# One more set of first-layer tiles by half products, and partial sums that grow in PSUM, in an attention and mixer kernel

## The chip, the core and the metric

The kernel runs on one core of one Trainium2 chip. The metric is device time in microseconds (us): the median of three runs is 332.39 us (332.39 to 332.7). A profiled execution of its own took 332.49 us, and its trace spans 330.7 us. TensorE multiplies (weights are loaded, then a matmul streams columns through them), VectorE, ScalarE and GpSimd work elementwise, SyncE issues DMAs. TensorE writes only to PSUM, which has eight banks of 512 f32 columns; GpSimd does not touch PSUM here.

## The reference: what is computed

Eight batches of 576 tokens and eight heads of 64 channels: causal attention, with 16 beacon keys ahead that every token sees; then a low-rank mix over the tokens, and a two-layer MLP over the channels.

```python
scores = scale * np.matmul(q, k_all.transpose(0, 1, 3, 2))
scores = np.where(causal, -1000000000.0, scores)
a = np.exp(scores - scores.max(-1, keepdims=True)); a /= a.sum(-1, keepdims=True) + 1e-09
x = np.matmul(a, v_all)                     # then (B, S, H * D): 8 x 576 x 512
u = x + ((x.transpose(0, 2, 1) @ U) @ V).transpose(0, 2, 1)
out = u + np.maximum(u @ w_ch1, 0.0) @ w_ch2   # 512 -> 2048 -> 512
```

## The kernel before

**Two streams of work.** The 4608 tokens are nine MLP blocks of 512 tokens, numbered 0 to 8; a block needs the mixed result `u` of the batch or batches that it lies in. Attention goes by pairs of heads. A *visit* makes scores (`sps`, L410: matmuls of 64 rows, two heads side by side) and ScalarE turns them into exponentials (L419); then come 15 matmuls per head against the values (`po`, L428), and VectorE takes the reciprocal of the sums (L436) and scales the head into `xb` (L437). After a batch's last head, DMA transposes and two small products (`qtp`, L465, four groups of 32 columns; `ups`, L490, 32 rows) make `u`, transposed, in the ring `uT`. MLP blocks are cut into *units* which wait in a queue; `fill(n)` takes `n` of them between pieces of attention. After the last batch the queue is emptied with no attention left.

**Who orders.** Nothing is scheduled: each engine carries out its instructions in the order in which the program issues them, and semaphores make it wait for operands and for buffers. PSUM tiles take the first bank of the list `emptied` (`pst`) and put it at the list's end when their last reader has been issued (`emptying`), so a bank is used again in the order in which banks were given back, and a matmul into it waits for that reader.

**A block.** The first layer has 16 output tiles `gT` of 128 channels by 512 tokens. A *plain* tile is four matmuls of 512 columns (`gps`, L675; in block 4, where the ring wraps, eight of 256) and a ReLU on ScalarE (L683) or VectorE (L681). A *set* makes four tiles (2q, 2q+1, 8+2q, 9+2q) at once by seven products of half channels by half tokens (a Strassen-Winograd scheme), each of four matmuls of 256 columns, 28 in all (`qps`, L701). Blocks 3 to 5 make one set, blocks 6 to 8 three (`PARTS`). The weights' sums for a set lie in freed staging tiles (`quad_weights`, L615, GpSimd); the sums of `u` are VectorE's (L603). In a set, bank A takes the first product, ScalarE copies it to SBUF (L720), A goes on to grow by the second, third and fourth product, with a copy after each; F takes a product alone and VectorE adds the copy (L723) and applies the ReLU (L728); D grows by two products and VectorE adds copies to it twice.

The second layer treats the whole block the same way: seven products of 16 matmuls of 256 columns, over sums of the tiles (`sums`, L653, VectorE). In blocks 1 to 6 products have banks A to F of their own (`product`, L829; A of blocks 3 to 6 by `grown`, L909), and VectorE adds each bank to the kept stage before it (`after`, L849); in blocks 7 and 8 one bank A grows. GpSimd adds `u` (L577), SyncE stores.

Of the kernel before, what the change touches and what calls it, by code (L numbers as in the profile page):

```python
# [11 lines left out]
F32 = mybir.dt.float32  # L12
# [6 lines left out]
P = 128  # L19
# [11 lines left out]
def kernel(  # L31
# [73 lines left out]
    bank_of = {}  # L105

    def pst(shape, dtype, name):

        b = emptied.pop(0)
        t = psum.tile(shape, dtype, tag=f"bank{b}", name=name)  # L110
        bank_of[id(t)] = (b, t)
        return t

# [467 lines left out]
    def quad_tiles(q):  # L581

        if q == 0:
            w = [pairs.tile([P, 512], F16, name=f"lw{k}", tag=f"pr{k % 2}") for k in range(4)]
        else:
            w = [staged[q - 1][:, ds(512 * k, 512)] for k in range(4)]
            f = staged[q + 1][:, 0 : 2048].bitcast(F32).rearrange("p (k i x) -> p k i x", k=2, i=2)
            lq["k", q] = (f[:, 0], f[:, 1], f[:, 0])
# [6 lines left out]
    def u_sums(t0, eng):  # L595

        b11, b12, b21, b22 = (u_half(t0, c, x) for c in (0, 2) for x in (0, HT))
        t1, t2, t3, t4 = (staged[i][:, 5 * DM : 6 * DM].rearrange("p (c x) -> p c x", c=2) for i in range(4))
        lq["t"] = [t1, t2, t3, t4]

        def one(o, x, y):
            assert (t0 + 511) // S in settled
            eng.tensor_tensor(out=o, in0=x, in1=y, op=ALU.subtract)  # L603
# [18 lines left out]
    def fast_units(t0, dst, last=False, parts=0, ahead=None):  # L622
# [3 lines left out]
        few = PARTS.get(t0 // 512 + 1, 0) == 1  # L626
# [3 lines left out]
        def begin():  # L630
            t = gtp.tile([P, NDC * 512 + 3 * HF * HT], F16, name="gT", tag="gT")
# [14 lines left out]
        def sums(i, d0, n):  # L646
# [6 lines left out]
            nc.vector.tensor_tensor(out=o[:, ds(d0, n)], in0=x[:, ds(d0, n)], in1=y[:, ds(d0, n)], op=op)  # L653

        order = [d + HF * h for d in range(HF) for h in range(2)]

        def g_unit(k):
            if k == 0:
                begin()


            def between():
                if k % 2 and cell["turns"]:
                    cell["turns"].pop(0)()
                for x in SUMS.get(k, ()):
                    sums(*x)

            layer_one(order[k], k in (2, 5, 11, 13), between)

        def layer_one(dc, on_vector, between=lambda: None):  # L670
# [8 lines left out]
            between()  # L679
            if on_vector:  # L680
                nc.vector.tensor_scalar_max(out=cell["g"][:, dc, :], in0=g, scalar1=0.0)  # L681
            else:
                nc.scalar.activation(out=cell["g"][:, dc, :], in_=g, func=AF.Relu)  # L683
            emptying(g)

        def g_quads():

            b11, b12, b21, b22 = (u_half(t0, c, x) for c in (0, 2) for x in (0, HT))
            us = u_sums(t0, nc.vector)
            t1, t2, t3, t4 = lq["t"]  # L690
            held = {}

            def plain(k, dc):
                layer_one(dc, parts == 1 and k in (2, 11, 13))

            def half(q, bank, a, b, fresh):
                if fresh:
                    held[q, bank] = pst([P, 2, HT], F32, name="qps" + bank)
                for i in range(2):
                    for c in range(2):  # L700
                        nc.tensor.matmul(  # L701
                            held[q, bank][:, i, :], a(c, i), b[:, c, :], start=fresh and i == 0 and c == 0,
                            stop=c == 1, skip_group_check=True,
                        )

# [3 lines left out]
            def of_lw(q, k):  # L709
                return lambda c, i: lq["w", q][k][:, c, ts(i, P)]  # L710

            def space(q, k):
                if k < 2:
                    cell["k", q, k] = lq["k", q][k] if q else kept("k")
                else:
                    cell["k", q, k] = cell["k", q, 0]
                return cell["k", q, k]

            def copied(q, k):
                nc.scalar.activation(out=space(q, k), in_=held[q, "A"], func=AF.Copy)  # L720
# [949 lines left out]
```

## Time and profile before

| what | number |
|---|---|
| median of three runs | 332.39 us |
| the profiled execution, and its span | 332.49 us, 330.7 us |
| TensorE busy | 322.6 us, 98% of the span, 3660 matmuls |
| VectorE busy | 264.7 us, 80% |
| ScalarE busy | 196.4 us, 59% |
| GpSimd busy | 166.7 us, 50% |
| granted TensorE clock, mean | 0.996 |
| plain tiles of 512 columns in blocks 1 to 8 (L675) | 272 matmuls, 66.3 us |

Busy shares are means over the span, and the end of a matmul is modelled. A row of the timeline gives the start, the length from the first start to the last end, the engine, line and operation, output and inputs, and a count; a row of the groups gives the count, the busy time and the mean length of one, and then the engine's idle time ahead of it with who ended it.

### The profile page before, as it was taken

The page shows a single profiled execution, that of the slowest core. Times are in us where ns is not written, and L with a number is a line of the kernel's source. Part 1 is how long each engine was busy: PE and PEld are TensorE (multiplying, and loading weights), DVE is VectorE, ACT ScalarE, POOL GpSimd, SP SyncE. Part 2 cuts the span into 40 slices and gives each one's busy share as a digit, 9 for nine tenths or more (in the row PEclk, how much of TensorE's full clock was granted, in tenths as well). Part 3 has the DMA queues.
Part 4 walks back from the last instruction along what each step waited for, and adds up shares of the span by engine and source line. Part 5 has one row for each costly group of instructions (what it writes and reads, how often), then busy time and mean ns, then how long its engine had stood idle before and what let it go on. Part 6 is the DMA issues. An engine that isn't in the chain of part 4 may idle for free.

```text
span 330.7 us, 9280 instructions
## 1 busy us (share of the span) xinstructions
PE 322.6 (98%) x3660; PEld 228.1 (69%) x3660; DVE 264.7 (80%) x608; ACT 196.4 (59%) x430; POOL 166.7 (50%) x263
## 2 busy tenths in 40 slices
PE   7899999999999999999999999999999999999994
PEld 3564555555578656876588888765787888788783
DVE  6776988679998668786878777877788898798993
ACT  5957962789972677348844695379636613703700
POOL 8987724766238960689058923950283036030030
PEclk9999999999999999999999999999999999999998
DMA  7999999999999996999999999995014313405003
GB/s 164 142 179 143 185 201 194 200 187 155 80 129 166 215 130 106 111 162 138 148 149 162 146 135 160 92 211 81 10 65 120 70 44 101 63 11 166 18 10 125
DMA packets 150561, 41.99 MB, mean 127 GB/s; under 512 B 131312, under 2 KB 149936, under 8 KB 150512
## 3 DMA queue, kind: packets, MB, share of 16 engines
q0 software_dynamic: 87568, 18.18, 73.1%
q1 hardware_dynamic: 62144, 22.41, 37.4%
q10 hardware_dynamic: 800, 0.75, 0.7%
q8 instruction: 30, 0.49, 0.7%
q14 instruction: 19, 0.16, 0.2%
HBM read 37.45 MB, written 9.44 MB: 142 GB/s over the span
## 4 chain that ended last, share of the span: by engine, by line
PE 91%; ACT 4%; DVE 1%; DMA 1%; issue 0%; ACTq 0%
PE gps L675 21%; PE mpsA L909 9%; PE po L428 8%; PE qpsA L701 6%; PE mpsD L829 6%; PE sps L410 6%; PE cps L1053 4%; PE gps L1027 4%; PE mpsE L829 3%; PE mpsC L829 3%; PE mpsB L829 3%; PE qpsD L701 3%; ACT expt L377 2%; PE mpsF L829 2%; PE mpsD L909 2%; ACT w L377 2%
## 5 line engine op out<-in xcount | busy, mean ns | idle before, releaser
L577 POOL TENSOR_TENSOR ob<-ob,ut 128x128 f32<-128x128 f32 x104 | 50.0, 511 | 121.9 <-DVE ob L849 59.4
L419 ACT ACTIVATE expt<-sps 128x496 f16<-128x496 f32 (+2 forms) x192 | 82.0, 539 | 41.8 <-PE sps L410 41.8
L675 PE MATMUL gps<-uT,w 128*128 128x512 f16 (+1 forms) x368 | 78.1, 351 | 0.0
L829 PEld LDWEIGHTS <-gT 128*128 128x128 f16 x576 | 54.2, 98 | 8.8 <-issue 2.6
L675 PEld LDWEIGHTS <-w 128*128 128x128 f16 x368 | 33.2, 98 | 25.6 <-issue 1.3
L653 DVE TENSOR_TENSOR gT<-gT 128x1024 f16<-128x1024 f16 (+3 forms) x87 | 47.0, 561 | 0.9
L239 POOL DMA_DIRECT2D vs<-in_v_dram x50 | 39.9, 811 | 14.1 <-DMA w<-in_moe_w_ch_dram 11.6
L683 ACT ACTIVATE gT<-gps 128x512 f16<-128x512 f32 x63 | 37.4, 617 | 16.1 <-PE gps L675 11.9
L428 PEld LDWEIGHTS <-expt 128*128 128x128 f16 x900 | 33.9, 98 | 8.4 <-issue 1.5
L428 PE MATMUL po<-vs,expt 128*128 128x65 f16 x900 | 36.4, 194 | 0.6 <-DVE expt L349 0.4
L909 PEld LDWEIGHTS <-gT 128*128 128x128 f16 x336 | 31.2, 98 | 4.0
L437 DVE TENSOR_TENSOR xb<-po,rec 128x320 f16<-128x320 f32 x64 | 31.4, 491 | 2.2
L349 DVE TENSOR_TENSOR expt<-expt,bigmask 128x768 f16<-128x768 f16 x56 | 31.3, 598 | 0.4 <-ACT expt L419 0.2
L720 ACT ACTIVATE kept<-qpsA 128x512 f32<-128x512 f32 x18 | 10.9, 603 | 24.0 <-PE qpsA L701 13.2
L410 PE MATMUL sps<-qT,kT 64*128 64x80 f16 (+4 forms) x288 | 22.6, 281 | 0.0
L436 DVE RECIPROCAL rec<-po 128x5 f32<-128x5 f32 x64 | 11.9, 186 | 12.4 <-PE po L428 12.1
L377 ACT ACTIVATE expt<-sps 128x496 f16<-128x496 f32 (+2 forms) x48 | 20.6, 572 | 0.6 <-PE sps L371 0.6
L909 PE MATMUL mpsA<-w,gT 128*128 128x256 f16 x160 | 19.1, 273 | 0.0
L410 PEld LDWEIGHTS <-kT 64*128 64x128 f16 x288 | 10.2, 94 | 12.8 <-issue 8.2
L681 DVE TENSOR_SCALAR gT<-gps 128x512 f16<-128x512 f32 x17 | 11.7, 688 | 8.5 <-PE gps L675 8.2
L1126 POOL DMA_DIRECT2D st<-in_k_dram x20 | 16.9, 860 | 1.4 <-DVE xb L437 1.4
L1126 POOL DMA_DIRECT2D st<-in_q_dram x20 | 17.0, 877 | 0.2 <-DVE expt L349 0.2
(159 smaller groups left out, 540.4 us busy)
## 6 DMA issues: line engine op xcount, KB each, us to landing
out_dram<-ob SPq DMA_DIRECT2D x33, 256.0 KB, 3.4
vs<-in_v_dram POOLq DMA_DIRECT2D x18, 128.0 KB, 7.2
w<-in_moe_w_ch_dram POOLq DMA_DIRECT2D x4, 512.0 KB, 6.6
w<-in_moe_w_ch_dram POOLq DMA_DIRECT2D x2, 1024.0 KB, 13.1
st<-in_k_dram POOLq DMA_DIRECT2D x12, 128.0 KB, 6.3
st<-in_q_dram POOLq DMA_DIRECT2D x12, 128.0 KB, 8.3
st<-in_k_dram POOLq DMA_DIRECT2D x4, 288.0 KB, 11.5
st<-in_q_dram POOLq DMA_DIRECT2D x4, 288.0 KB, 12.5
```

The costliest lines, as they stand in the source:

```text
L239: nc.gpsimd.dma_start(out=dst[a : a + nq[j], j, :, :], in_=src[hs, ds(q0[j], nq[j]), :].rearrange("h p d -> p h d"))
L377: nc.scalar.activation(out=ex[i][:, ds(AT[g], gw[g])], in_=ps[g, i][:, 0 : gw[g]], func=AF.Exp, scale=scale)
L410: nc.tensor.matmul(banks[i][:, ds(at0 + o, w)], kT(hp, c, ch), qT[hp, c, ds(qa, w)], start=True, stop=True, skip_group_check=len(unit) > 1,)
L419: nc.scalar.activation(out=at[p][3][i][:, ds(AT[g], gw[g])], in_=bank[:, ds(at0, gw[g])], func=AF.Exp, scale=scale)
L428: nc.tensor.matmul(po[:, j, :], ex[0 : nk[c], ds(blk[(c, j)], P)], vs[0 : nk[c], ds(c * H * E + h * E, E)], start=(c == 0), stop=(c == j),)
L577: nc.gpsimd.tensor_tensor(out=o[:, i, ds(c, w)], in0=x[:, i, ds(c, w)], in1=y[:, i, ds(c, w)], op=op)
L653: nc.vector.tensor_tensor(out=o[:, ds(d0, n)], in0=x[:, ds(d0, n)], in1=y[:, ds(d0, n)], op=op)
L675: nc.tensor.matmul(g[:, ds(o, w)], w1[:, cc, ts(dc, P)], uT[:, cc, ds(at, w)], start=(cc == 0 and o == 0), stop=(cc == NCC - 1), skip_grou ...
L683: nc.scalar.activation(out=cell["g"][:, dc, :], in_=g, func=AF.Relu)
L829: nc.tensor.matmul(ps, a()[:, d, ds(P * i, P)], bm[:, d, ds(c0, w)], start=fresh and d == 0 and i == 0, stop=d == HF - 1, skip_group_check ...
L909: nc.tensor.matmul(ps, a()[:, d, ds(P * i, P)], bm[:, d, ds(c0, w)], start=fresh and d == 0, stop=d == HF - 1, skip_group_check=True,)
L1126: coming.append(lambda d=dst, s=src, a=m[j] - nq[j], n=m[j], j=j: nc.gpsimd.dma_start(out=d[a:n, j, :, :], in_=s[:, ds(q0[j], nq[j]), :].r ...
```

## The change

1. **Sets.** Blocks 3 to 5 make sets 0 and 3, blocks 6 to 8 make all four. Set 3 keeps its weight sums in the quarter of `w2` (first half of the rows, second half of the columns) that nothing reads after block 0; the rarely taken general branch loads that quarter again.
2. **Seeds.** `pst(..., onto=True)` takes a free bank that matmuls have filled whole before. ScalarE copies the first product of A into it and F's product is added onto it there, so VectorE's addition is gone. Where no such bank is free, the old way stays. In the program as built this holds for 13 of 18 sets and for the second layer of blocks 1 to 6.
3. **Second layer of blocks 1 to 6.** One bank A grows by four products, as blocks 7 and 8 do; ScalarE copies whole stages of 512 columns out of A to the output tiles, D is added to them by VectorE. B, C and E are gone.
4. **Order.** A table of words per block (`PLANS`) gives each unit its steps, the sums, the transposes and the engine of each copy or ReLU; a table per batch (`SLOTS`) gives the order of attention and units from batch 3 on.

```diff
+    def pst(shape, dtype, name, onto=False):
+        n = next(i for i, b in enumerate(emptied) if b in filled) if onto else 0
+        b = emptied.pop(n)
...
+            def a(q, eng):
+                x = half(q, "A", of_w1(0, 2 * q), b11)
+                if seedable():
+                    held[q, "F"] = pst([P, 2, HT], F32, "qpsF", True)
+                copy(eng, held[q, "F"] if (q, "F") in held else space(q, 1), x)
+            def f(q, eng):
+                onto, c11 = (q, "F") in held, low(2 * q)
+                x = half(q, "F", of_w1(2, 2 * q), b21)
+                if not onto:
+                    summed(c11, x, k[q, 1])
+                relu(eng if onto else "v", c11, x if onto else c11)
+                freed(q, "F")
+            def b(q, eng):
+                copy(eng, space(q, 0), half(q, "A", of_lw(q, 1), t2))
+            def d(q, eng):
+                half(q, "D", of_lw(q, 0), t1)
+            def c(q, eng):
+                copy(eng, space(q, 1), half(q, "A", of_lw(q, 2), t3))
+                summed(high(HF + 2 * q), held[q, "D"], k[q, 1])
+            def e(q, eng):
+                relu(eng, low(HF + 2 * q), half(q, "A", of_w1(2, HF + 2 * q), t4))
+                freed(q, "A")
+            def g(q, eng):
+                summed(high(2 * q), half(q, "D", of_lw(q, 3), b22), k[q, 0])
+                freed(q, "D")
...
-            elif k == 2:
-                add(kept("u2"), banks["B"], cell["s1"])
-                freed("B")
...
+            def one(i):
+                grown(0, "A", i, 0, HC)
+                if i:
+                    cell["onto"] = seedable()
+                    if cell["onto"]:
+                        banks["F"] = pst([P, 2, HC], F32, "mpsF", True)
+                    copied(banks["F"] if cell["onto"] else kept("s1"), "A")
+            def six(i):
+                grown(2, "A", i, 0, HC)
+                if i:
+                    copied(out_tile("12"), "A")
...
-    PARTS = {3: 1, 4: 1, 5: 1, 6: 3, 7: 3, 8: 3}
+    PLANS = {
...
+            g1 | e0 r0 | r1s | g2 +0.0.4 | d3 c3 +1.1.1 t1 e2 t1 | r2p +1.0.1 | e1 m0 e3 t1 g3 r3 | m1 +0.4.2
...
+    SLOTS = {
...
+            t f v1:2,1:1,1:0 y f f a0 b0 f f m1 v2:0,2:1,2:2 l f f f a1 f y f y b1 f f f L f f v2:3,3:0,3:3,3:1
```

The order lists three places on which the prediction speaks. A `MATMUL` row stands here for all that are like it; rows between are left out at "...".

First, TensorE at the end of the fourth batch, in block 3 (`gT_2940` before, `gT_2934` now): the last head `po`, twelve score matmuls, and what follows. Before:

```order
L428 MATMUL po_3099<-vs0_111,expt3_108 128x65
L410 MATMUL sps0_3122<-qT_2559,kT1_110 128x336
...
L410 MATMUL sps1_3135<-qT_2559,kT1_110 128x208
L675 MATMUL gps_3148<-uT_102,w1_93 128x512
L675 MATMUL gps_3154<-uT_102,w1_93 128x512
```

Now:

```order
L436 MATMUL po_3092<-vs0_111,expt3_108 128x65
L418 MATMUL sps0_3115<-qT_2557,kT1_110 128x464
...
L418 MATMUL sps1_3126<-qT_2557,kT1_110 128x80
L704 MATMUL qpsA_3144<-uT_102,w1_93 128x256
L704 MATMUL qpsD_3151<-st0_113,w2_94 128x256
L685 MATMUL gps_3156<-uT_102,w1_93 128x512
```

A plain tile stood behind the scores; now the new set's first product stands there, and the bank that it takes is the one of the head just ahead, so its first weight load waits for VectorE's `xb`. Blocks 4 and 5 have the same place.

Second, TensorE where the last set's bank A grows, in block 6. Before (third set, `qpsA_5020`):

```order
L701 MATMUL qpsA_5020<-st1_114 128x256
L675 MATMUL gps_5049<-uT_102,w1_93 128x512
L701 MATMUL qpsA_5020<-st2_115,st1_114 128x256
L701 MATMUL qpsD_5061<-st0_113,st1_114 128x256
L909 MATMUL mpsA_5068<-w2_94,gT_4835 128x256
L701 MATMUL qpsA_5020<-st3_116,w1_93 128x256
L701 MATMUL qpsD_5061<-uT_102,st1_114 128x256
```

Now (set 3, `qpsA_5052`; the fourth product of set 2, `qpsA_4939`, lies between):

```order
L704 MATMUL qpsA_5052<-st1_114,w2_94 128x256
L704 MATMUL qpsF_5057<-uT_102,w1_93 128x256
L704 MATMUL qpsA_5052<-st2_115,w2_94 128x256
L818 MATMUL mpsA_5094<-w2_94,gT_4851 128x256
L704 MATMUL qpsA_4939<-st3_116,w1_93 128x256
L704 MATMUL qpsD_5059<-uT_102,w2_94 128x256
```

Between the second and the third product into A stood a plain tile of 512 columns; now four matmuls of 256 stand there. In block 4 it is the mixer's `qtp` that stands at this place:

```order
L704 MATMUL qpsA_3804<-st1_114,w2_94 128x256
L473 MATMUL qtp_3856<-xb_3226,Usb_95 32x128
L704 MATMUL qpsA_3804<-st2_115,w2_94 128x256
L685 MATMUL gps_3886<-uT_102,w1_93 128x256
L436 MATMUL po_3897<-vs0_111,expt0_105 128x65
```

Before, those twenty `qtp` came straight behind a visit of scores.

Third, ScalarE in the second layer of block 3. Before, with both halves of a stage copied apart:

```order
L919 ACTIVATE kept_3296<-mpsA_3287 128x256
L919 ACTIVATE kept_3296<-mpsA_3299 128x256
L419 ACTIVATE expt0_105<-sps0_3311 128x496
...
L419 ACTIVATE expt1_106<-sps1_3320 128x496
L926 ACTIVATE ob_3341<-mpsA_3287 128x256
L926 ACTIVATE ob_3341<-mpsA_3299 128x256
```

Now:

```order
L893 ACTIVATE mpsF_3321<-mpsA_3301 128x512
L427 ACTIVATE expt0_105<-sps0_3327 128x496
...
L427 ACTIVATE expt1_106<-sps1_3340 128x464
L893 ACTIVATE ob_3366<-mpsA_3301 128x512
L893 ACTIVATE ob_3454<-mpsA_3301 128x512
L893 ACTIVATE ob_3465<-mpsF_3321 128x512
```

The first stage is now copied whole and into PSUM, ahead of the six exponentials of the visit that stands between the first and the second product into A; three more stages of A and F follow as copies of ScalarE.

563 lines of the change are left out of this document (259 added, 304 removed), and 3 rows, old and new, of the table SUMS.

## The prediction

> **What bounds the kernel now.** I read the page's first, second and fourth parts, and then asked the trace for TensorE's waits.
>
> ```profile
> PE 322.6 (98%) x3660; PEld 228.1 (69%) x3660; DVE 264.7 (80%) x608; ACT 196.4 (59%) x430; POOL 166.7 (50%) x263
> PE   7899999999999999999999999999999999999994
> PE 91%; ACT 4%; DVE 1%; DMA 1%; issue 0%; ACTq 0%
> PE idle L274 <- DVE ones L159: 1.2, 1, 1.2
> PE sps L371 <- DVE qT L332: 0.5, 1, 0.5
> PE tps L299 <- DVE pr L292: 0.5, 2, 0.3
> PE po L428 <- DVE expt L349: 0.4, 1, 0.4
> PE po L428 <- DVE w L349: 0.2, 1, 0.2
> ```
>
> TensorE is busy in every slice but the first and the last, it holds 91% of the chain, and all its waits that are long enough to be listed come to 2.8 us in lines that run in the first two batches. Busy alone proves little, because matmul ends are modelled: a wait under about 0.16 us can hide in the tail of the matmul before. So I looked at the steps between matmuls in the timeline.
>
> ```profile
> 121.31 3.63 PE L675 MATMUL gps<-uT,w 128*128 128x512 f16 x16
> 163.85 1.91 PE L909 MATMUL mpsA<-w,gT 128*128 128x256 f16 x16
> 165.69 0.79 PE L410 MATMUL sps<-qT,kT 64*128 64x496 f16 x10
> 166.42 0.28 PE L909 MATMUL mpsA<-w,gT 128*128 128x256 f16 x1
> L675 PE MATMUL gps<-uT,w 128*128 128x512 f16 x272 | 66.3, 379 | 0.0
> L909 PE MATMUL mpsA<-w,gT 128*128 128x256 f16 x160 | 19.1, 273 | 0.0
> ```
>
> Sixteen matmuls of 512 columns take 3.63 us and the last of them 0.379, so one follows another after (3.63 - 0.379) / 15 = 0.2167 us. For 256 columns it is (1.91 - 0.273) / 15 = 0.1091. Such stretches stand back to back. Two things follow. Work taken off TensorE is worth its full price, and TensorE is already at its own pace, so the kernel can gain no more than that work; any wait that the new order brings is a plain loss.
>
> **What is removed.** One set more in each of blocks 3 to 8. A set replaces four plain tiles, 16 matmuls of 512 columns, by seven half products, 28 matmuls of 256: 16 x 0.2167 - 28 x 0.1091 = 3.467 - 3.055 = 0.41 us. In block 4 the ring wraps, and the four tiles are 32 matmuls of 256: 0.44. The program's order counts the same: 80 matmuls of 512 and 32 of 256 go, 168 of 256 come. 5 x 0.41 + 0.44 = **2.5 us less**. Second-layer products keep their number.
>
> **What the order adds on TensorE: changes of form.** Scores use 64 rows, the mixer's qtp 32 columns, its ups 32 rows. After the mpsA above, the last matmul starts at 163.85 + 1.91 - 0.27 = 165.49 and the scores at 165.69: 0.20 instead of 0.11. A change of form costs 0.09 us. Where two such stretches touch, one change is saved, as here:
>
> ```profile
> 124.87 0.79 PE L410 MATMUL sps<-qT,kT 64*128 64x496 f16 x10
> 125.59 0.47 PE L465 MATMUL qtp<-xb,Usb 112*32 112x128 f16 x20
> 125.99 0.39 PE L675 MATMUL gps<-uT,w 128*128 128x512 f16 x1
> ```
>
> The old order has six such neighbours (five of scores and qtp, one of scores and ups), the new one two. Four changes more: **+0.4 us**.
>
> **What it adds as waits.** The partial sums stay in one bank while ScalarE copies them, so the next product into that bank waits for the copy. Its price comes from these rows:
>
> ```profile
> 262.65 0.60 PE L701 MATMUL qpsA<-st,w 128*128 128x256 f16 x4
> 263.28 0.60 ACT L756 ACTIVATE gT<-qpsA 128x512 f16<-128x512 f32 x1
> L720 ACT ACTIVATE kept<-qpsA 128x512 f32<-128x512 f32 x18 | 10.9, 603 | 24.0 <-PE qpsA L701 13.2
> 261.60 0.59 ACT L720 ACTIVATE st<-qpsA 128x512 f32<-128x512 f32 x1
> 262.22 0.69 DVE L723 TENSOR_TENSOR gT<-qpsD,st 128x512 f16<-128x512 f32 x1 [0.29 <-ACT st L720]
> 12.00 0.76 DVE L332 COPY qT<-tps 128x576 f16<-128x576 f16 x1 [0.57 <-PE tps L305]
> 12.81 0.38 PE L371 MATMUL sps<-qT,kT 64*128 64x496 f16 x2 [0.51 <-DVE qT L332]
> ```
>
> ScalarE starts 0.03 after the matmul's end, takes 0.60, VectorE follows ScalarE after 0.03, and TensorE starts 0.05 after the engine that it waits for. From the start of the last matmul into a bank to the first that may write there again: 0.27 + 0.03 + 0.60 + 0.05 = 0.95 us, if ScalarE is free. I compare that with the TensorE work which the new order puts between.
>
> (a) Block 6, set 3: between the second and the third product into A stand the four matmuls of F alone. 5 x 0.109 = 0.55, so **0.40** of wait. Behind it the copy of the third is added into D's part by VectorE before D's last product: 0.27 + 0.03 + 0.60 + 0.03 + 0.69 + 0.05 = 1.67 against 13 steps of 0.109 = 1.42: **0.25** more. The old order had four matmuls of 512 columns at the first of these places and sixteen of 256 at the second.
>
> (b) Block 4, set 3: only the twenty qtp stand between.
>
> ```profile
> 266.25 1.80 PE L829 MATMUL mpsB<-wt,gT 128*128 128x256 f16 x15
> 267.98 0.47 PE L465 MATMUL qtp<-xb,Usb 112*32 112x128 f16 x20
> 268.38 1.92 PE L829 MATMUL mpsC<-wt,gT 128*128 128x256 f16 x16
> ```
>
> From the last start, 266.25 + 1.80 - 0.27 = 267.78, to 268.38 is 0.60: **0.35** of wait. (In blocks 3 and 5 scores cover that place.)
>
> (c) Second layer, blocks 1 to 5: the first product's copy into F's bank lies behind one visit of scores. Ten score matmuls, as at 165.49 to 166.42, give 0.93 against 0.95: 0.02 in each of four blocks, **0.08**. Block 1 has six:
>
> ```profile
> 94.22 1.91 PE L829 MATMUL mpsA<-w,gT 128*128 128x256 f16 x16
> 96.06 0.67 PE L410 MATMUL sps<-qT,kT 64*128 64x208 f16 x6
> 96.66 1.05 PE L829 MATMUL mpsF<-w,gT 128*128 128x256 f16 x8
> ```
>
> 94.22 + 1.91 - 0.27 = 95.86 to 96.66 is 0.80: **0.15**. Its price as a copy into PSUM is not in the trace; the nearest rows write SBUF at 0.60, and I take that; were it 0.1 shorter or longer, these five would sum to 0.05 or 0.73.
>
> By the Trainium skill (ScalarE: Activation LUTs, its remark in the part on the activation pipeline), ScalarE is faster into PSUM than into SBUF; Perfetto Trace Analysis, Optimizing Scalar/DVE Operations, gives 51 against 93 ns of overhead, with about twice that in a profiled duration. An estimate from it: 0.08 us less a copy, which leaves 0.07 of the 0.23 under (c) and makes the forecast 332.0. No row here has such a copy.
>
> (d) Blocks 3, 4 and 5: after the last head of a batch come twelve scores and then set 3's first product, which takes the bank of that head. The bank is free when VectorE has normalised the head.
>
> ```profile
> 120.06 0.63 PE L428 MATMUL po<-vs,expt 128*128 128x65 f16 x15
> 120.62 0.76 PE L410 MATMUL sps<-qT,kT 64*128 64x336 f16 x12
> 120.77 0.18 DVE L436 RECIPROCAL rec<-po 128x5 f32<-128x5 f32 x1
> 120.98 0.49 DVE L437 TENSOR_TENSOR xb<-po,rec 128x320 f16<-128x320 f32 x1
> 121.31 1.25 PE L675 MATMUL gps<-uT,w 128*128 128x512 f16 x5
> ```
>
> Here the head ends at 120.69, the bank is free at 121.47, and 0.05 later TensorE could have it: 0.83 after the head. The same twelve scores are over 0.62 after it. Now nothing needs that bank so soon; then it costs 0.21, three times: **0.63**.
>
> (a) to (d): 0.65 + 0.35 + 0.23 + 0.63 = 1.9 us. Ends: none of it if the owners are released before these rows say, and about 2.7 if ScalarE or VectorE is busy when the bank is ready.
>
> **What lies beside other work.**
>
> ```profile
> 262.85 0.39 ACT L919 ACTIVATE kept<-mpsA 128x256 f32<-128x256 f32 x1 [0.66 <-PE mpsA L909]
> vs<-in_v_dram POOLq DMA_DIRECT2D x18, 128.0 KB, 7.2
> ```
>
> By the order ScalarE gains 59 instructions of 512 elements and four of 1024, and loses 27 of 512 and 16 of 256: 32 x 0.60 - 16 x 0.39 = 13, with up to 1.2 for each of the four 17 us, which takes it from 59 to 65% of the span. VectorE loses 32 operations of 512 elements (among them the 18 that added B, C and E) and gains 26: six fewer, about 4 us at 0.69. GpSimd gains four weight sums and one ReLU. All of it lies under TensorE's time; with that cover gone, ScalarE's 17 us would be added. The DMAs are as many as before on every queue, and are issued elsewhere in the same batch: a load lands 7.2 us after its issue and is used in the next batch, so that I price the move at nothing; were one load late by its whole landing, that would be the price.
>
> **Sum.** The profiled run: 332.49 - 2.5 + 0.4 + 1.9 = 332.3; it lies 0.1 above the median of 332.39, so the forecast is **332.2 us**.
>
> **Rivals.** *Faster.* The four banks come free earlier than these rows say, or waits overlap with each other and with the drain of a change of form. For it: the old order never waits after the second batch, so rows of a waiting TensorE there do not exist, and a wait late in a block gives all later ones slack. Against it: each price is a sum of shown rows with the engine taken as idle. With 0.5 us of waits: 332.39 - 2.5 + 0.4 + 0.5 = 330.8. It decides below 1.4 us of waits in all.
>
> *Slower: ScalarE's queue.* ScalarE takes instructions in order, and copies now stand between exponentials.
>
> ```profile
> 121.10 1.51 ACT L419 ACTIVATE expt<-sps 128x496 f16<-128x496 f32 x3 [0.24 <-PE sps L410]
> 150.00:160.00 10.00, 10.00 (x99) 5.45 (x100) 5.96 (x13) 8.66 (x20) 7.72 (x10) 1.00 1.69 148
> 190.00:200.00 10.00, 10.00 (x132) 8.30 (x130) 7.85 (x19) 8.47 (x20) 2.05 (x3) 1.00 2.40 144
> ```
>
> Exponentials follow each other after (1.51 - 0.60) / 2 = 0.46 us, and in these stretches of ten, where ScalarE's column is the fourth busy time, it is already at 8.5 to 8.7. If one copy into A in each of blocks 3 to 6 stands behind one exponential more than I count, TensorE waits 4 x 0.46 = 1.8 longer: 334.0. It decides from 0.9 us on top of my 1.9. By Perfetto Trace Analysis, Matmuls, independent groups should rotate through banks so that evacuation overlaps the next group; growing sums in A does the reverse, and (a) and (b) are such places.
>
> *That it does not do what it says:* a seed is used only if a filled bank is free when the program is built. The order lists six seeded second layers (blocks 1 to 6) and 13 of 18 sets; the others keep VectorE's sum. Nothing is left open there.
>
> **Chances.** 0.2% is 0.66 us, about what a measurement of this kernel can tell from no change; no change is 331.7 to 333.05. The forecast with waits of 1.4 to 2.7 us: 0.45. The faster rival: 0.37. The slower: 0.18. The forecast's own range is 331.7 to 333.0; with both rivals' nearer parts, 330.6 to 333.5 holds eight in ten.
>
> **What would show it.** In the new profile TensorE's 512-column rows fall by 80 and the span without waits by about 2. The list of TensorE's waits must show qpsA waiting for VectorE's xb three times and for ScalarE's kept in blocks 4 and 6, 0.2 to 0.4 each. If that list stays as short as now, the faster rival is right; if qpsA or mpsA waits for ScalarE at more places, or longer than 0.5, the slower. A long wait for VectorE in the last two blocks, or for a DMA, would be a mechanism that I have not priced.

## The result, and the profile after

The changed kernel takes 340.08 us (median of 6 runs, 339.82 to 340.98) beside 332.49 us for the kernel before (median of 6): a ratio of 1.0228, 95% interval 1.0204 to 1.0253. It is slower by 7.6 us, where 332.2 was forecast. The profiled execution took 339.87 us.

The page of the changed kernel: busy times, and the chain.

```profile
PE 324.2 (96%) x3716; PEld 235.1 (69%) x3716; DVE 266.9 (79%) x608; ACT 210.5 (62%) x450; POOL 174.3 (52%) x268
...
PE 80%; DVE 11%; ACT 6%; issue 1%; ACTq 0%; DVEq 0%
```

Busy shares hardly moved (VectorE was at 80%, and is at 79%). The chain did: VectorE held 1% of it and now holds 11%. Where that stands is told by the list of TensorE's waits in the changed kernel (total in us, times, longest):

```profile
PE qpsA L704 <- DVE kept L670: 1.8, 1, 1.8
PE idle L282 <- DVE ones L167: 1.2, 1, 1.2
PE po L436 <- DVE expt L357: 1.1, 3, 0.4
PE qtp L473 <- DVE gT L678: 0.8, 1, 0.8
PE mpsA L818 <- DVE gT L666: 0.8, 1, 0.8
PE qpsA L704 <- ACT kept L672: 0.6, 2, 0.3
...
PE qpsD L704 <- DVE gT L730: 0.2, 1, 0.2
```

Only the idle row and a part of the po row were there before. The rest is new, nearly all of it is for VectorE, and much of it for operations that the change did not add: masks (`expt`, L357), sums and ReLUs of `gT` (L666, L678).

Runs of one kernel differ by 1 to 3.5 us (332.06 to 334.07 for the six of the kernel before). So I compare, beside the medians, one stretch of the one trace that each kernel has: from the start of block 1's first plain tile to the start of the last row of products. First the two rows in the trace of before, then in that of after:

```profile
70.67 1.89 PE L675 MATMUL gps<-uT,w 128*128 128x512 f16 x8
...
324.12 1.93 PE L909 MATMUL mpsD<-w,gT 128*128 128x256 f16 x24
```

```profile
71.12 1.89 PE L685 MATMUL gps<-uT,w 128*128 128x512 f16 x8
...
331.25 1.93 PE L818 MATMUL mpsD<-w,gT 128*128 128x256 f16 x24
```

324.12 - 70.67 = 253.45 us before, 331.25 - 71.12 = 260.13 after: 6.68 of the 7.6 us lie in this stretch. It seems a steady measure: a variant of the kernel before, below, has 253.45 as well, though its median is 0.2 us away and its profiled run 1.9, so that there the difference lies ahead of block 1. How far the stretch varies from run to run of one kernel is not known.

**Where the masks go wrong.** One line per kernel of the view of one tile, the masks on `expt`: count, then shortest, median and longest in ns. Before, then after:

```profile
L349 DVE TENSOR_TENSOR expt<-expt,bigmask x56: 537/550/1498, 34.7 to 254.6; 128x768 f16<-128x768 f16 x56
```

```profile
L357 DVE TENSOR_TENSOR expt<-expt,bigmask x56: 540/549/2400, 35.2 to 260.2; 128x768 f16<-128x768 f16 x56
```

The operation is the same and so is its median. Some take up to four times as long. The timeline of the changed kernel around its longest wait shows beside what (GpSimd, then VectorE, then TensorE):

```profile
195.96 1.22 POOL L628 TENSOR_TENSOR st<-w 128x512 f16<-128x512 f16 x1
197.26 1.36 POOL L628 TENSOR_TENSOR st<-st,w 128x512 f16<-128x512 f16 x1
198.59 1.46 POOL L628 TENSOR_TENSOR st<-w 128x512 f16<-128x512 f16 x1
200.02 1.20 POOL L628 TENSOR_TENSOR st<-w,st 128x512 f16<-128x512 f16 x1
...
196.48 2.56 DVE L357 TENSOR_TENSOR expt<-expt,bigmask 128x768 f16<-128x768 f16 x2 [0.17 <-ACT expt L427]
198.96 0.68 DVE L730 TENSOR_TENSOR gT<-qpsF,kept 128x512 f16<-128x512 f32 x1
...
200.13 1.23 DVE L666 TENSOR_TENSOR gT<-gT 128x256 f16<-128x256 f16 x1
...
201.49 0.67 DVE L670 COPY kept<-qpsA 128x512 f32<-128x512 f32 x1
...
202.21 0.60 PE L704 MATMUL qpsA<-st,w 128*128 128x256 f16 x4 [1.84 <-DVE kept L670]
```

While GpSimd makes the weights' sums of a set, two masks take 2.56 us in place of 2 x 0.55, and a sum of 256 elements 1.23 (0.52 in w_chained, below; the shortest of its kind takes 0.27). The addition at 198.96, with one operand in PSUM, keeps its 0.68. The copy that TensorE waits for stands behind all of this in VectorE's queue: 1.46 + 0.96 = 2.4 us late, and TensorE waits 1.84. The same four GpSimd sums stand beside the waits at 98 to 101 us (0.75 for a sum, and about 0.5 more at a copy of keys and queries and at a mask), 129.90 (0.79) and 228.04 (0.43): one place for each of the four sets; 4.3 us in all. At 228 they are not alone: the mask, the one of 2.40 us, began beside the pieces of GpSimd's residual.

### The profile page after: what moved, and what is told of

It is laid out like the page before. It is cut to its first block, busy times and chain, and to the rows that moved or that the text cites. A ratio compares the mean times of both kernels' runs of the same rounds, so it can differ in the third digit from the quotient of the medians.

```text
span 338.2 us, 9395 instructions
## 1 busy us (share of the span) xinstructions
PE 324.2 (96%) x3716; PEld 235.1 (69%) x3716; DVE 266.9 (79%) x608; ACT 210.5 (62%) x450; POOL 174.3 (52%) x268
## 4 chain that ended last, share of the span: by engine, by line
PE 80%; DVE 11%; ACT 6%; issue 1%; ACTq 0%; DVEq 0%
PE mpsA L818 15%; PE gps L685 11%; PE qpsA L704 8%; PE mpsD L818 8%; PE po L436 7%; PE sps L418 5%; PE qpsD L704 4%; PE cps L1023 4%; PE gps L997 4%; DVE expt L357 3%; PE mpsF L818 3%; ACT expt L385 2%; DVE gT L666 2%; PE qpsF L704 2%; PE tps L307 1%; DVE xb L445 1%
## 5 line engine op out<-in xcount | busy, mean ns | idle before, releaser
L685 PE MATMUL gps<-uT,w 128*128 128x512 f16 (+1 forms) x256 | 54.7, 352 | 0.0
L666 DVE TENSOR_TENSOR gT<-gT 128x256 f16<-128x256 f16 (+5 forms) x99 | 50.3, 544 | 1.2 <-ACT gT L676 0.9
L818 PE MATMUL mpsA<-wt,gT 128*128 128x256 f16 x384 | 46.9, 273 | 0.8 <-DVE gT L666 0.8
L357 DVE TENSOR_TENSOR expt<-expt,bigmask 128x768 f16<-128x768 f16 x56 | 37.6, 709 | 8.4 <-ACT expt L427 8.4
L676 ACT ACTIVATE gT<-gps 128x512 f16<-128x512 f32 x44 | 26.9, 617 | 16.2 <-PE gps L685 15.4
L704 PEld LDWEIGHTS <-w 128*128 128x128 f16 x312 | 29.6, 98 | 9.2 <-issue 3.7
L685 PEld LDWEIGHTS <-w 128*128 128x128 f16 x256 | 23.4, 98 | 17.6 <-DVE pr L300 0.4
L893 ACT ACTIVATE ob<-mpsA 128x512 f32<-128x512 f32 x18 | 11.4, 632 | 26.7 <-issue 13.2
L730 DVE TENSOR_TENSOR gT<-qpsD,kept 128x512 f16<-128x512 f32 x24 | 16.5, 687 | 4.6 <-ACT kept L672 2.3
L704 PE MATMUL qpsA<-st,w 128*128 128x256 f16 x120 | 17.5, 272 | 2.4 <-DVE kept L670 1.8
L485 DVE TENSOR_TENSOR uT<-ups,uT 128x496 f16<-128x496 f32 x24 | 14.5, 666 | 4.9 <-PE ups L498 4.9
```

The costliest lines, as they stand in the source:

```text
L357: nc.vector.tensor_tensor(out=e, in0=e, in1=bigmask[:, :, :].rearrange("p (a b) x -> p a b x", b=2), op=ALU.min)
L666: eng.tensor_tensor(out=o[:, ds(d0, n)], in0=x[:, ds(d0, n)], in1=y[:, ds(d0, n)], op=op)
L685: nc.tensor.matmul(g[:, ds(o, w)], w1[:, cc, ts(dc, P)], uT[:, cc, ds(at, w)], start=(cc == 0 and o == 0), stop=(cc == NCC - 1), skip_grou ...
L704: nc.tensor.matmul(held[q, name][:, i, :], a(c, i), b[:, c, :], start=fresh and i == 0 and c == 0, stop=c == 1, skip_group_check=True,)
L818: nc.tensor.matmul(ps, a()[:, d, ds(P * i, P)], bm[:, d, ds(c0, w)], start=fresh and d == 0, stop=d == HF - 1, skip_group_check=True,)
```

## The experiments

Three theories stood at the start. **G**: GpSimd's work holds VectorE's operations up, and the new order has put weight sums beside operations that TensorE soon needs. **Q**: the new order runs VectorE's queue too tightly, whoever lengthens it. **S**: ScalarE's queue and the growing banks cost the time (the prediction's slower rival). All results in one table; the stretch is worked out from the two rows as above.

| kernel | median us | ratio to before, 95% | stretch us |
|---|---|---|---|
| before | 332.4 to 332.7 | 1 | 253.45 |
| changed | 340.08 | 1.0204 to 1.0253 | 260.13 |
| w_on_vector | 335.56 | 1.0064 to 1.0098 | 256.13 |
| w_pieces | 349.76 | 1.0489 to 1.0531 | 271.62 |
| w_chained | 335.19 | 1.0046 to 1.0107 | 255.68 |
| copies_on_scalar | 342.65 | 1.0244 to 1.0387 | 262.86 |
| before_w_on_vector | 332.84 | 0.9981 to 1.0029 | 253.45 |
| before_pieces | 333.43 | 1.0012 to 1.0078 | 254.38 |
| no_set3 | 337.88 | 1.0082 to 1.0178 | 257.68 |
| no_seeds | 341.92 | 1.0207 to 1.0306 | 261.87 |
| gaps | 337.27 | 1.0078 to 1.0164 | 257.01 |
| block6_spaced | 335.27 | 1.0056 to 1.0097 | 254.70 |
| best_try | 334.30 | 1.0029 to 1.0067 | 254.54 |

### Who carries out the weight sums

**w_on_vector**, in the changed kernel:

```diff
-            lambda o=o, x=x, y=y, op=op: nc.gpsimd.tensor_tensor(out=o, in0=x, in1=y, op=op)
+            lambda o=o, x=x, y=y, op=op: nc.vector.tensor_tensor(out=o, in0=x, in1=y, op=op)
```

> The changed kernel, with the sixteen sums of weights (quad_weights, 128x512 f16) issued at the same places of the program but carried out by VectorE and not by GpSimd; nothing else differs. Theory G (GpSimd stretches VectorE): in the changed kernel a mask of VectorE takes 0.55 us alone and 1.5 to 2.4 us where a weight sum runs beside it, and TensorE's new waits for VectorE at 98 to 101, 202 and 228 to 231 us stand right behind such stretched operations; they come to about 0.8 + 0.7 + 1.9 + 0.9 = 4.3 us. Then this kernel takes 335 to 337, and the masks near 196 and 226 us go back to 0.55. Theory Q (VectorE's queue is ordered too tightly, whoever lengthens it): the four sums in a row are 4 x 0.42 = 1.7 us on VectorE in place of a stretch of about 2.5, the waits stay at over half their size and the time is 338.5 to 340. Theory S (ScalarE's queue and the growing banks cost the time): no change, 340.

335.56 us, and the stretch is 4.00 shorter, as G had it. VectorE now carries out sixteen operations more, and TensorE waits for it less; Q is out as the main cause. The waits at 98, 130 and 202 us are gone from the list. The one at 228 is not, and its mask did not go back to 0.55 as expected: it takes 2.47 us, beside the residual alone.

**before_w_on_vector** is the same edit in the kernel before.

> The kernel before, with its twelve weight sums on VectorE and not on GpSimd. There two masks are stretched by them too (0.72 and 1.50 us at 115 us), but TensorE waits for none. Theory G: nothing is won where the stretch has slack: 332 to 333. Theory Q: twelve more operations of 0.42 us in VectorE's queue cost waits: 333 to 335. If VectorE as the place of these sums were better whatever the order, 331.5 or less.

332.84 us, interval 0.9981 to 1.0029, and the stretch is the same to the hundredth. The old order held masks up as well (1498 ns above) and TensorE waited for none of them. So the new cost needs both: the collision, and an order in which the result is needed at once.

**copies_on_scalar** takes copies of bank A off VectorE's queue, three in each of blocks 3 to 5 and two in block 6:

```diff
-            ... c0v 11 | ... t1 a3v | ... | c3v 13
+            ... c0 11 | ... t1 a3 | ... | c3 13
-            ... | d0 f1v b0v | t1 t1 b1v
+            ... | d0 f1v b0 | t1 t1 b1
```

> The changed kernel, with five copies of bank A per use of the order tables (words c0v, a3v, c3v in blocks 3 to 5, b0v and b1v in blocks 6 to 8's table entry for block 6) on ScalarE and not on VectorE. Theory G: the longest wait of TensorE (1.8 us at 202 us, for VectorE's copy that is queued behind two stretched masks and a stretched sum) goes, the other new waits stay: 338 to 338.7. Theory Q: VectorE is relieved of eleven operations of 0.69 us, all new waits for VectorE shrink: 336 to 338. Theory S: ScalarE gets eleven more copies of 0.60 us ahead of exponentials: 340.5 to 342.

342.65 us. G's number for it was wrong by 4 us, S's was the nearest. TensorE's waits in it:

```profile
PE qpsA L704 <- ACT kept L672: 2.9, 6, 0.9
PE po L436 <- DVE expt L357: 1.6, 3, 1.0
```

The wait for VectorE's copy is gone, and there are six waits for ScalarE's copies, 2.9 us, where the changed kernel has two, 0.6: the copies queue behind exponentials and ReLUs. The mechanism of the prediction's slower rival exists; the changed kernel avoids most of it by giving these copies to VectorE, and that put them behind the masks.

### What holds VectorE: a stream without a gap

**w_pieces** cuts each weight sum into four pieces of 128 columns, on GpSimd.

```diff
-            lambda o=o, x=x, y=y, op=op: nc.gpsimd.tensor_tensor(out=o, in0=x, in1=y, op=op)
+            lambda o=o, x=x, y=y, op=op: in_pieces(o, x, y, op)
```

> The changed kernel, with each of the sixteen weight sums cut into four pieces of 128 columns, still on GpSimd. Theory G, if VectorE is kept out for as long as one instruction of GpSimd runs: a VectorE operation waits for a quarter (about 0.3 us) and then gets its turn, the masks beside the sums take about 0.8 and not 1.5 to 2.4, most of the 4.3 us come back: 336 to 337.5. If the two engines only share bandwidth evenly, the stretch depends on how long GpSimd works and not on the pieces: 339.5 to 340.5. Theories Q and S: 340.

Both versions of G were wrong here: 349.76 us, 9.7 more than the changed kernel. The tile view and the timeline of w_pieces (VectorE, GpSimd, TensorE):

```profile
L357 DVE TENSOR_TENSOR expt<-expt,bigmask x56: 536/552/5169, 35.5 to 272.0; 128x768 f16<-128x768 f16 x56
```

```profile
200.66 5.87 DVE L357 TENSOR_TENSOR expt<-expt,bigmask 128x768 f16<-128x768 f16 x2
...
204.61 2.20 POOL L585 TENSOR_TENSOR st<-w,st 128x128 f16<-128x128 f16 x4
...
233.35 5.53 DVE L357 TENSOR_TENSOR expt<-expt,bigmask 128x768 f16<-128x768 f16 x2
...
234.89 1.56 POOL L585 TENSOR_TENSOR st<-w 128x128 f16<-128x128 f16 x4
236.43 1.56 POOL L585 TENSOR_TENSOR st<-w,st 128x128 f16<-128x128 f16 x4
...
238.47 0.63 PE L436 MATMUL po<-vs,expt 128*128 128x65 f16 x15 [3.09 <-DVE expt L357]
238.93 3.26 PE L685 MATMUL gps<-uT,w 128*128 128x512 f16 x8
```

GpSimd's pieces follow each other without a gap (four in 1.56 us). The first of the two masks at 233.35 takes 5.06 us and ends only behind the last piece; the one at 200.66 takes 5.17 and gets its turn behind the fourteenth of sixteen (so that the last four, at 204.61, last 2.20 us and not 1.56). Either is passed over at the ends of twelve pieces, so it is not held for one instruction of GpSimd. Of the whole sums, the second needs the first just ahead of it, which makes a gap: in the timeline of the changed kernel above, 0.08 us from the end of the first sum at 197.18 to the second. The pieces need one that is four or more pieces back, so there are no gaps. That was a story from two traces, so I tried it.

**w_chained** has the same 64 pieces as w_pieces, in another order (a counter of finished quarters is left out here):

```diff
...
+        def quarter(c, x):
+            for o, a, b, op in (
+                (s1, a21, a22, ALU.add), (s2, s1, a11, ALU.subtract),
+                (s4, a12, s2, ALU.subtract), (s3, a11, a21, ALU.subtract),
+            ):
+                at = ds(P * x, P)
+                nc.gpsimd.tensor_tensor(out=o[:, c, at], in0=a[:, c, at], in1=b[:, c, at], op=op)
...
+        return [lambda c=c, x=x: quarter(c, x) for c in range(2) for x in range(2)]
```

> The changed kernel with its sixteen weight sums on GpSimd in the same 64 pieces of 128 columns as in w_pieces (349.76 us), only in another order: the four sums of one quarter stand together, first, second, fourth, third, so that the second needs the first just ahead of it and the fourth the second. At each such place GpSimd has to wait for its own result. If a VectorE operation is held until GpSimd's stream has such a gap, it is held for three pieces at most (about 1.3 us) and mostly for one: no mask takes 5 us, most are under 1.3, and the time is 336 to 339. If the number of pieces or GpSimd's work as such made w_pieces slow, 347 to 350.

335.19 us: 14.6 less than w_pieces with the same operations on the same engine, and a little better than expected. A part of the 14.6 is the half clock that the waits of w_pieces brought on (last section). Its timeline (GpSimd, then the same two masks as at 196.48 above):

```profile
193.10 0.49 POOL L635 TENSOR_TENSOR st<-w 128x128 f16<-128x128 f16 x1
193.67 0.75 POOL L635 TENSOR_TENSOR st<-st,w 128x128 f16<-128x128 f16 x1
194.50 0.63 POOL L635 TENSOR_TENSOR st<-w,st 128x128 f16<-128x128 f16 x1
...
193.58 1.26 DVE L357 TENSOR_TENSOR expt<-expt,bigmask 128x768 f16<-128x768 f16 x2 [0.17 <-ACT expt L427]
...
195.68 0.52 DVE L671 TENSOR_TENSOR gT<-gT 128x256 f16<-128x256 f16 x1
```

With gaps of 0.08 us behind the first and the second piece two masks take 1.26 and not 2.56. A gap lets VectorE in. It is not the only thing that does: the mask at 200.66 in w_pieces got its turn between two pieces where the profile shows no gap, and so did the second mask at 196.48 in the changed kernel, which ends at 199.04, 0.42 behind the second whole sum, with the third already begun. What ends a hold there is open.

**gaps** tries the same on GpSimd's other work, the residual (with the weight sums on VectorE): a copy of one column onto itself, which has to wait for the piece, behind each piece.

```diff
+                last = o[:, i, ds(c + w - 1, 1)]
+                nc.gpsimd.tensor_copy(out=last, in_=last)
```

> The changed kernel with the weight sums on VectorE (335.56 us), and behind each of the 104 pieces of the residual on GpSimd a copy of one column onto itself, which has to wait for the piece, so that GpSimd's stream has a gap after every piece. In the kernel with pieces of weight sums a mask began beside a stream of sixteen pieces and ended only when the stream did (5.17 us). If a VectorE operation of f16 that finds GpSimd at work is held until GpSimd's stream has a gap, the masks of 2.1 and 2.5 us beside the residual fall to 1.1 or less, the waits behind them (0.32 + 0.67 + 0.29) go, and the time is 334.2 to 334.8. If the two engines share the path evenly while both work, the longer stream only stretches more: 335.6 to 336.5.

```profile
L357 DVE TENSOR_TENSOR expt<-expt,bigmask x56: 539/551/780, 36.6 to 258.5; 128x768 f16<-128x768 f16 x56
```

```profile
PE sps L418 <- DMA qT<-st: 2.2, 2, 1.4
...
PE po L436 <- DMA vs<-in_v_dram: 0.6, 1, 0.6
...
PE po L436 <- DVE expt L357: 0.4, 1, 0.4
```

The mechanism came out as expected: no mask takes over 0.78 us (2.47 in w_on_vector), and two of three waits for masks are gone. The time did not: 337.27, 1.7 more, of which 0.9 lie in the stretch. TensorE now waits for loads (2.2 us in the stretch). GpSimd also issues loads, and the 104 copies lengthen its queue; that this makes the loads late is argued from the list, not tested. A gap is worth having where GpSimd has nothing urgent behind it.

**before_pieces** puts the stream of pieces into the kernel before.

> The kernel before, with its twelve weight sums cut into pieces of 128 columns on GpSimd, so that the stream of GpSimd beside the masks at 115 us has no gap for 16 pieces (6.7 us). Theory G (a VectorE operation of f16 that meets GpSimd's stream is held until it has a gap): a mask there takes 4 to 7 us in place of 0.72 and 1.50, TensorE waits for it at the next head: 335 to 339. If it is the new order alone that makes waits (theory Q or S), 332 to 333.

333.43 us, 0.9 more in the stretch, far under the 335 to 339 expected. The masks at 115 us take 0.74 and 0.78 there: the first stood in VectorE before the first weight piece came, and the two engines then took turns (pieces of 0.75 us beside the masks, 0.42 alone). Sums of `u` and `gT` were held, up to 3.15 us, and TensorE waited for little of it. So a stream without a gap does not always hold VectorE. When VectorE is held and when the two take turns is open.

### The prediction's own terms

These start from w_on_vector (335.56 us, stretch 256.13).

**block6_spaced** moves products in block 6 and one ReLU in block 7:

```diff
-            ... d3 +1.0.3 e1 g2 b3 | f3 r2 | c3 m0 ... | +1.3.1 e2 | g3 r3 | +0.6.2 m1 e3 | m4
+            ... d3 +1.0.3 e1 b3 | f3 g2 r2 | c3 m0 ... | +1.3.1 e2 | e3 g3 r3 | +0.6.2 m1 | m4
-            ... t1 e2 t1 | r2p +1.0.1
+            ... t1 e2 t1 | r2v +1.0.1
```

> The changed kernel with the weight sums on VectorE (335.56 us), and two places more: in block 6 another product of four matmuls (g of set 2) stands between the second product of set 3 into bank A and the third, and e of set 3 stands ahead of its g, so that each copy has four matmuls more of cover; in block 7 the ReLU of set 2 (1.45 us on VectorE's queue mate GpSimd, behind which a sum waits) is VectorE's. If step (a) of the prediction is right (0.40 + 0.25, and 0.41 + 0.27 in the trace) and the wait of 0.39 in block 7 is GpSimd's, both places run without a wait and the time is 335.56 - 0.68 - 0.39 = 334.5. If such waits only move to the next product, 335.3 to 335.8.

The median fell by 0.3, with runs from 334.24 to 336.34; the stretch fell by 1.43, in a profiled run (334.25) that is among the fastest. The waits of step (a) and the one in block 7 are gone from its trace; a wait of 0.3 for the copy into the second layer's F came instead, and a mask that took 2.47 us at 221 us no longer met GpSimd's stream. The time of one place cannot be had from the median alone.

**no_set3** makes tiles 6, 7, 14 and 15 plain again (here the words of blocks 3 to 5; those of 6 to 8 likewise).

```diff
-            ... t1 a3v | d3 5 | e0 | f3v +1.0.1 t1 b3 | c3v 13 | e3 | t1 g3 +0.4.1 r3
+            ... t1 6 | 5 | e0 | 7 +1.0.1 t1 | 14v 13 | | t1 15 +0.4.1
```

> The changed kernel with the weight sums on VectorE (335.56 us), and set 3 undone in blocks 3 to 8: its tiles 6, 7, 14 and 15 are plain tiles again, and its four weight sums are left away; seeds, grown banks and the order of the rest stay. By the prediction's own terms TensorE gets 2.5 us of work back, and the waits (a), (b) and (d), in the trace 0.68 + 0.38 + 0.59 = 1.65, go: 336.4. If set 3 costs more than these waits (its copies and sums crowd VectorE and ScalarE for all that follows), 335.5 or less; if the waits stay because the new order makes them, 338.

337.88 us, next to the third forecast; in the stretch 1.55 more, between the first and the third. Set 3 is worth something once its weight sums are off GpSimd's stream, about 1.5 of the 2.5 us of work that it takes off TensorE. By the prediction's terms it would be 2.5 less the 1.6 of waits, 0.9; no_set3 has two new waits for the copy into the second layer's F instead, 0.3 and 0.2.

**no_seeds** puts the first product's copy into SBUF and the addition back on VectorE (`seedable` always says no). Where the order has the third copy ahead of F's addition, that copy overwrites the first one, so that in those sets F's sum is taken from other values; the operations are as many.

> The changed kernel with the weight sums on VectorE (335.56 us), and no seeds: the copy of the first product goes to SBUF and VectorE adds it to F's product, as in the kernel before (13 sets and six second layers; 19 additions of 0.69 us come back to VectorE, the ReLUs of the 13 sets move there as well). If step (c) (0.23 us of waits for the copy into F's bank) is all that the seeds cost and VectorE has room, 335.3. Theory Q (VectorE's queue is what the order lives on): new waits for VectorE, 337 to 339.

341.92 us, 5.7 more in the stretch, with waits for masks (2.7), for ScalarE's copies (1.9) and for VectorE's sums (1.8). The order was made for seeds, and here F waits for a later copy than it would need, so the size is no price of the seeds; that undoing them saves nothing is shown. Q may have this much truth, that VectorE's queue has no room for nineteen additions more; the later copy keeps this run from showing it.

**best_try** adds to block6_spaced a plain tile of cover in blocks 3 to 5, another place for block 6's first second-layer product, and one gap in block 2's residual:

```diff
-            ... d3 5 | e0 | f3v +1.0.1 t1 b3 | c3v 13 ...
+            ... d3 | e0 | f3v +1.0.1 t1 b3 5 | c3v 13 ...
-            ... | e3 g3 r3 | +0.6.2 m1 | m4
+            ... | m1 g3 r3 | +0.6.2 e3 | m4
```

> The kernel of block6_spaced (weight sums and block 7's ReLU on VectorE, block 6 spaced) with three places more: in blocks 3 to 5 the plain tile 5 stands between the second and the third product of set 3 into bank A (step (b), 0.38 in the trace); in block 6 the first product of the second layer stands ahead of set 3's last, and its e behind, so that each copy is covered (0.34); and the GpSimd stream of block 2's third residual has one gap, behind its second piece, beside the mask of 2.1 us (0.31 and 0.29 of wait behind it). Without these waits the stretch from block 1's first plain tile to the last matmul falls from 256.40 to about 255.1, which is that of the kernel before (255.16): 332.3 to 333.7 in the median. If waits like (a) and (b) only move on to the next product, 335.

334.30 us: the best of the new order, and still slower than the kernel before by 0.3 to 0.7%. The stretch came down by 0.16 only, to 254.54, 1.1 above before.

## Why the prediction was wrong

**The bound, right.** TensorE at its own pace, so that any wait is a plain loss. That is why 4.3 us of held VectorE came through in full.

**The work removed, right.** The plain tiles among the changed kernel's groups:

```profile
L685 PE MATMUL gps<-uT,w 128*128 128x512 f16 x192 | 46.7, 379 | 0.0
```

272 plain matmuls of 512 columns have become 192, 80 fewer as counted.

**Waits (a), (b) and (d): right to a few hundredths.** TensorE's rows of the changed kernel for (a), then those for (b) and (d):

```profile
267.26 0.60 PE L704 MATMUL qpsF<-uT,w 128*128 128x256 f16 x4
268.11 0.60 PE L704 MATMUL qpsA<-st,w 128*128 128x256 f16 x4 [0.25 <-ACT kept L672]
...
269.42 0.60 PE L704 MATMUL qpsA<-st,w 128*128 128x256 f16 x4
270.12 0.60 PE L704 MATMUL qpsD<-uT,w 128*128 128x256 f16 x4
```

```profile
197.67 0.47 PE L473 MATMUL qtp<-xb,Usb 112*32 112x128 f16 x20
198.45 0.60 PE L704 MATMUL qpsA<-st,w 128*128 128x256 f16 x4 [0.31 <-ACT kept L672]
...
159.33 0.76 PE L418 MATMUL sps<-qT,kT 64*128 64x464 f16 x12
160.22 0.61 PE L704 MATMUL qpsA<-uT,w 128*128 128x256 f16 x4
```

(a): the last matmul of F starts at 267.26 + 0.60 - 0.27 = 267.59, A at 268.11: 0.52, less one step of 0.11 is 0.41 (forecast 0.40); then 270.12 - 269.75 - 0.11 = 0.26 (0.25), with 269.75 the start of the last matmul of the row before. (b): from 197.67 to 198.45 is 0.78, where the same step took 0.40 before: 0.38 (0.35). (d): 0.89 from the scores to the product, 0.69 before: 0.20 (0.21), and about as much in the other two blocks. These three kinds come to 1.6 us, and the sum had 1.63.

**Wait (c): there, and mis-sized.** Block 2's place (TensorE's product and scores, ScalarE's copy, TensorE again), and the copies' groups:

```profile
134.05 0.82 PE L818 MATMUL mpsA<-w,gT 128*128 128x256 f16 x6
134.80 0.79 PE L418 MATMUL sps<-qT,kT 64*128 64x496 f16 x10
...
134.96 0.58 ACT L893 ACTIVATE mpsF<-mpsA 128x512 f32<-128x512 f32 x1 [2.12 <-PE mpsA L818]
...
135.59 1.25 PE L818 MATMUL mpsA<-wt,gT 128*128 128x256 f16 x10
```

```profile
L672 ACT ACTIVATE kept<-qpsA 128x512 f32<-128x512 f32 x18 | 10.8, 602 | 1.4 <-PE qpsA L704 1.3
...
L672 ACT ACTIVATE qpsF<-qpsA 128x512 f32<-128x512 f32 x13 | 7.4, 591 | 14.4 <-PE qpsA L704 13.3 <-DVE ob L785 1.1
```

From the scores' start to the next product is 0.79, where ten scores took 0.73 before: 0.06, and 0.07, 0.11 and 0.06 in blocks 3 to 5; block 1 has 0.24 (0.84 for six scores, 0.60 before), where a score also waits for VectorE's `xb`. Together 0.54 in place of 0.23. The product ends at 134.87 and ScalarE starts 0.09 later, not 0.03: the hand-over was taken from one row that was too good. The copy into PSUM was taken as 0.60 and is 0.59. What the Trainium skill says (ScalarE: Activation LUTs, Step-by-step: what each stage is for), that ScalarE is faster into PSUM than into SBUF, the trace bears out, with 591 against 602 ns; my estimate of 0.08 from the overheads in its Perfetto Trace Analysis (Optimizing Scalar/DVE Operations) is far off.

**The step that failed: "What lies beside other work".** GpSimd's four weight sums and one ReLU were counted, and put at nothing because they lie under TensorE's time. Their own time does; what they do to VectorE does not. The price belonged with the moves too: the new order issues all four sets' sums beside masks and sums that TensorE waits for at once. It came to 4.0 to 4.5 us (w_on_vector, w_chained). VectorE was to be busy 4 us less and is busy 2.2 more, with 608 operations as before and not six fewer: the masks alone take 37.6 us where they took 31.3. ScalarE's part of the sum was near, 17 us (its terms give 17.8) against 14.1. The ReLU in block 7 had a price of its own: a sum took 1.45 us beside it, and a product waited, 0.39 by its step. The trace of before had the sign: one mask at 1498 ns among 56 with a median of 550. Nothing in the argument asked for the longest of a group; the group's mean, 598 ns, hides it. By the Trainium skill (SBUF — State Buffer, Who interferes with whom and Summary) a VectorE operation with two SBUF inputs contends with a GpSimd one that reads SBUF, and the second to issue is blocked until the first finishes. The trace agrees on who is hit: masks and `gT` sums are, the addition with a PSUM operand is not. It differs on how long: beside the pieces of w_pieces a mask was passed over at the ends of twelve instructions.

**The rivals.** The faster one fell: the waits (a) to (d) came at 2.1 us, more than the 1.9 forecast. The slower one named the wrong queue for the changed kernel, though copies_on_scalar shows that it would have been right with those copies on ScalarE. Its 334.0 lies 1.2 to 1.6 us under what is left without GpSimd's part (335.2 to 335.6); that it comes so near is luck, since other waits make up that rest. The last sentence of the prediction, a long wait for VectorE as a mechanism not priced, is what happened, only from block 1 on and not in the last two blocks.

**What stays open.** 6.7 us in the stretch are -2.5 of work, +0.4 of changes of form, +2.1 of (a) to (d), 4.0 to 4.5 of weight sums, and about 0.7 at other waits for VectorE beside GpSimd's residual and ReLU (0.31 at 149 us, 0.39 in block 7). That makes 4.7 to 5.2, and leaves 1.5 to 2 us.

The trace tells where they lie. Set each step from one matmul's start to the next one's beside the usual step (the lower quartile over these traces) between the same two forms. In the kernel before no step of the stretch is over 0.15 us too long. In the changed kernel 17 are, by 8.4 us together: 5.6 at the weight sums' four places, 1.6 at (a), (b) and (d), 0.7 beside the residual and the ReLU, 0.3 at 151 us, where ScalarE's copy into F's bank waits 1.09 for VectorE's addition that reads that bank last, and 0.2 at (c). The list shows less because it counts a wait from the modelled end of the matmul before: 1.84 for a step that is 2.00 too long. Of the 5.6, w_on_vector and w_chained gave back 4.0 to 4.5. At the fourth place, 228 to 231 us, where the changed kernel's steps are 0.60 and 0.37 too long, w_on_vector still has 0.67 and w_chained 0.62 and 0.54, beside the residual; and w_on_vector has a new wait for `xb`, 0.44. No run takes the residual out, so its price is open.

## What to carry to other kernels

Before moving work between or past VectorE and GpSimd, ask for the longest instance of each VectorE group, not the mean: a few long ones beside GpSimd's stream are a cost that waits for an order in which they matter. If GpSimd has to make several small sums, try an order in which each needs the one before, or give VectorE the work; cutting them into independent pieces cost 9.7 us here, and 0.9 of the stretch in the kernel before. Waits that were worked out from rows (producer's end, copy, hand-over) came true to a few hundredths, but for (c), whose hand-over rested on one row; what was missed by most had been put at nothing.

## What the hardware showed that I had not expected

**A VectorE operation on f16 in SBUF can be held past many of GpSimd's instructions**: a mask takes 0.55 us alone, 0.78 where the two take turns, 5.17 beside sixteen pieces without a gap. With gaps of 0.08 us no mask that meets the weight sums alone takes over 0.78 (w_chained).

**Waits that lie close together, or a long one, cost twice.** After the wait of 3.09 us in w_pieces, eight matmuls of 512 columns took 3.26 us (from 238.93), where eight took 1.89 at full pace: (3.26 - 0.38) / 7 = 0.41 us apart and not 0.217. Two stretches of the same kernel (length, then busy times by engine, granted clock, DMA share, GB/s):

```profile
118.00:128.00 10.00, 9.54 (x83) 4.72 (x82) 9.33 (x11) 6.32 (x15) 9.99 (x21) 1.00 1.62 136
...
132.00:135.40 3.40, 3.40 (x12) 1.29 (x11) 0.88 (x2) 0.00 (x0) 0.00 (x0) 0.50 1.57 93
```

The granted clock goes to half at 130 us, within three waits of 1.03, 0.46 and 1.35 us that lie between 127.5 and 131.1, and stays there to 136.9; at two later places, behind waits of 2.06 and 1.99 and behind the one of 3.09, it is at half for 3.4 us. The Trainium skill (TensorE: Matmul & The Clock Gate, What's actually happening) has a window of about 3.4 us, and these lengths fit it: 6.8, 3.4 and 3.4. The changed kernel's waits, 1.84 us at most, did not bring this on: its clock is 0.999. Where the limit lies was not tried.
